# Pooled attention and two MoE layers on one core: which block of the expert stage follows its condition

## The chip, the core and the metric

The kernel runs on one core of one Trainium2 chip. The metric is the device time of one execution in microseconds; several runs are timed and their median is given. A profile is one further execution, recorded by the hardware profiler: its span runs from the first to the last instruction of the program.

## The reference, cut to what matters

Three stages follow one another. Attention with keys and values that are averaged over groups of 8, a dense layer with squared ReLU, and a layer of 8 experts: each of 2304 tokens goes to the expert with the largest logit, up to a capacity of 576 tokens for each expert, and its row is written with a gate weight.

```
logits = x @ w_gate
expert_idx = np.argmax(logits, axis=1)
...
h = np.maximum(np.einsum('ecd,edf->ecf', disp, w1), 0.0)
y = np.einsum('ecf,efd->ecd', h, w2)
...
        out[i] = gate_w[i] * y[expert_idx[i], pos[i]]
```

How many tokens an expert gets is known only when the routing has run, so the program has code for every outcome and picks its way by conditions on registers.

## The kernel before, in words

Attention and the dense layer are planned by a list of steps with priorities (class `Steps`, up to `S_.run()`); they run in 9 chunks of 256 tokens and fill most of the time. The expert stage behind them is written out by hand, in a fixed order on TensorE (PE), VectorE (DVE) and ScalarE (ACT).

An expert is worked in pieces. `fetch` takes the token numbers of a piece from a table and `gather` (L1002) issues an indirect DMA on GpSimd (POOL) for each 128 rows. `y_trans` (its transposes are L1030, its gate copy L1023, its two copies out of PSUM L1032 and L1033) turns the gathered rows into the layout that the multiplications need. `pair` multiplies 256 rows by the first matrix (L1470), applies ReLU, multiplies by the second matrix (`gb`, L1439) and ends in `finish`, which scales the rows and scatters them to the output by an indirect DMA on POOL (`put`, L1428). `trio` is `pair` with 64 rows more, `twins` (L1581 to L1639) takes two small experts at once. `w_load` issues the loads of the next expert's weights on the sync engine (SP, L1066), 7 loads of 512 KB in a row; ACT and DVE split them into two parts (L260, L261).

The first pair of the first expert stands ahead of the condition. It is cut in two: the call `second = pair(0, ..., cut=True)` issues everything up to the first quarter of the second output tile, and returns `second()`, which issues the remaining three quarters, beginning with a `y_trans(0)`. During the first part the routing of the last chunk ends: `finalize` and `line_index` compute the registers, the latter the one at place `R_LINE`, which is 1 when the counts of all experts fit the pattern for which `line()` was written.

Then every engine loads that register (`val`, L993) and branches on it (L1826). Where it is 1 the **straight code** runs: `second()`, a `trio`, and `line()`, which has two small conditions of its own (L1787). Otherwise the **general code** runs: `second()` and `rest()`, a deep tree of conditions with a block for each outcome. With the inputs of this case the straight code runs. Each engine has its own instruction stream in which all these blocks lie one behind another; the general code's are the many, the straight code's the few. `tc.If` takes as `preferred_fallthrough_block` which of its two blocks is laid directly behind the branch. Behind both is the end of the program: SP waits for the last DMAs, each engine drains, and a barrier of all engines closes it (the records with L1902).

Of the kernel before, what the change touches and what calls it, by code (L numbers as in the profile page):

```python
# [43 lines left out]
R_LINE = R_MAX + 1  # L44
# [184 lines left out]
def tile_kernel(ctx: ExitStack, tc: tile.TileContext, q, k, v, w_in, w_out, w_gate, w1, w2, cap, gate_rows, consts, out):  # L229
# [761 lines left out]
    def val(t, i, lo, hi, engines=None):  # L991
        kw = {} if engines is None else {"engines": engines}
        return nc.values_load(t[0:1, i:i + 1], min_val=lo, max_val=hi, **kw)  # L993
# [76 lines left out]
    def w_load(t, r, parts=range(NSTG), after=None):  # L1070

        if after is not None:
            for i in parts:
                nc.vector.tensor_copy(out=st["stg"][i][0:1, 0, 0:1], in_=f(after[0:1, 0, 2 * P - 1:2 * P]))
        e = r if t is None else val(t, r, 0, E - 1, SPE)
        for i in parts:
            w_part(e, i)
# [320 lines left out]
    mp, yg, yh, yl, cur, regs, regse = (st[x] for x in ("mp", "yg", "yh", "yl", "cur", "regs", "regse"))  # L1398
# [259 lines left out]
    def run(kind, r, x, nxt=True, split=None, n=2, part=range(16), extra={}, at=None, third=2):  # L1658

        if at is None:  # L1660
            at = x + 1 if kind is trio else x
        ft = [lambda: fetch(val(regs, 2 * E + r * NU + at, 0, E * NJ - 1, DVE), n, third)]
        sp = [] if split is None else split_list(split, 1 if kind is single else None)
        if kind is not single:
            h = {}
            for i in part if sp else ():
                h.setdefault(SPLITS[i], []).append(sp[i])
            nh = {0: ft, **{(11 if kind is trio else 8) + t: [lambda t=t: y_trans(t)] for t in range(n)}}
        else:
            h = {i: [sp[x] for x in part if a <= x < b] for i, (a, b) in enumerate(zip((0, *SINGLE), (*SINGLE, 16))) if sp}  # L1670
            nh = {0: ft, 4: [lambda: y_trans(0)]}
            if n > 1:
                nh[5] = [lambda: y_trans(1)]
        kind(r % 2, merged(nh if nxt else {}, h, extra))
# [65 lines left out]
    def rest():  # L1740

        nh = halves(0)
        with tc.If(val(regse, 2, 0, 1) < 1):
            with tc.If(nh > 0):
                fetch(val(regse, 1, 0, E * NJ - 1, DVE))
                y_trans(0)
                y_trans(1)
                with tc.If(nh > 2) as two:
                    run(pair, 0, 0, n=3)
                with two.Else():  # L1750
                    run(single, 0, 0)
        w_load(regs, 1)
        with tc.If(nh < 7) as three:
            with tc.If(nh > 4) as odd:
                run(single, 0, 1, True, 1)
            with odd.Else():
                for fn in split_list(1):
                    fn()
        with three.Else():
            many(nh, 0)  # L1760
        any_(1)
        overflow()
# [19 lines left out]
    def line():  # L1782


        for r in (1, 2):
            now = splits(r + 1, {h: [i for i in range(16) if SPLITS[i] == h] for h in range(16)} if r == 1 else W_REST)
            with tc.If(halves(r) > 8, preferred_fallthrough_block=False) as half:  # L1787
                run(trio, r, 0, at=0, extra=now, third=4)
            with half.Else():
                run(pair, r, 0, extra=now)  # L1790
            if r == 1:
                rows = {0: [next_rows(2, 3)], 8: [lambda: y_trans(0)], 9: [lambda: y_trans(1)], 10: [lambda: y_trans(2)]}
            else:
                rows = {0: [two_rows], 8: [y_two]}
            pair(r % 2, merged(rows, splits(r + 2, W_LATE, r == 1)))
        twins(splits(4, W_LAST, False))
# [15 lines left out]
    def ordered(*more):  # L1812
        return tc.manual_schedule(engines={ET.PE, *more})
# [9 lines left out]
            14: [lambda: y_trans(2)],  # L1823
        }, cut=True)
    with ordered(ET.DVE, ET.Activation):
        with tc.If(val(regs, R_LINE, 0, 1) > 0, preferred_fallthrough_block=False) as on:  # L1826
            second()
            run(trio, 0, 1, True, 1, 3, extra={0: [lambda: w_load(regs, 1)]}, third=4)
            line()
        with on.Else():  # L1830
            second()
            rest()
# [74 lines left out]
```

## Time and profile before

| | us |
|---|---|
| median of 3 runs | 683.26 |
| lowest and highest run | 681.84, 683.71 |
| the profiled execution, its own time | 682.42 |
| its span, first to last instruction | 680.7 |
| mean granted TensorE clock | 0.996 of full speed |

The first number is what a change is measured by. The profiled execution is one run; its own time is 1.7 us more than its span, and 0.84 us under the median. Its rows have a time axis that begins at the first instruction. PE is the matmul part of TensorE, PEld its weight loads; a "q" behind an engine's name (PEldq, POOLq) marks records of its sequencer, such as branches, waits and DMA issues, which don't count as busy time. `<-issue` behind an idle time means that the engine waited for no semaphore that the profile shows.

### The profile page before, as it was taken

To read this page: it belongs to the slowest core of one execution; us is meant where nothing else is said; L and a number is where in the kernel's file an instruction comes from. 1 tells how busy PE (TensorE), PEld (TensorE's weight loads), DVE (VectorE), ACT (ScalarE), POOL (GpSimd) and SP (SyncE) were. 2 spreads that over 40 slices of the span, in tenths; PEclk is the share of its full clock that TensorE was granted. 3 is DMA by queue.
4 is the path that set the end of the run, shared out by engine and by line. 5 is a ranking of instruction groups with operands and counts; after the bars stand their busy time and mean duration, and the time that the engine had idled before them with its cause. 6 is when DMAs were issued, how large, how long until landed. Compare 5 with 4: busy or idle time off the path is not lost. (4 is left out here: it accounts for less than half of the span.)

```text
span 680.7 us, 12008 instructions
## 1 busy us (share of the span) xinstructions
PE 666.2 (98%) x4263; PEld 599.2 (88%) x4264; DVE 418.5 (61%) x1127; ACT 328.2 (48%) x904; POOL 195.8 (29%) x230
## 2 busy tenths in 40 slices
PE   7999999999999999999999999999999999999996
PEld 6888889999999999889899899998997989889985
DVE  6998996222188899485379658445354466464352
ACT  5998884344254244354344333243431466453352
POOL 3524543232235233234233133242202211301110
PEclk9999999999999999999999999999999999999999
DMA  8989913010321220010010000062004674655110
GB/s 309 401 321 355 313 61 104 32 48 16 124 63 50 87 78 9 1 55 17 2 48 17 1 32 1 3 221 91 1 33 161 222 245 140 211 153 182 48 59 4
DMA packets 40682, 73.47 MB, mean 108 GB/s; under 512 B 8417, under 2 KB 17889, under 8 KB 40480
## 3 DMA queue, kind: packets, MB, share of 16 engines
q1 hardware_dynamic: 38208, 64.89, 28.1%
q0 software_dynamic: 2400, 7.66, 3.4%
q8 instruction: 38, 0.62, 0.4%
q14 instruction: 36, 0.29, 0.1%
HBM read 59.63 MB, written 13.12 MB: 107 GB/s over the span
## 5 line engine op out<-in xcount | busy, mean ns | idle before, releaser
L735 PE MATMUL h<-xh,W 128*128 128x256 f32 x1152 | 213.6, 284 | 0.4 <-ACT r L740 0.4
L755 POOL TENSOR_TENSOR gl<-r,gh 128x256 fp32r<-128x256 f32 x144 | 117.7, 818 | 271.6 <-ACT gh L751 161.3
L735 PEld LDWEIGHTS h<-xh,W 128*128 128x128 f32 x1152 | 184.3, 189 | 9.9 <-ACT r L740 0.6
L768 PE MATMUL y<-W,gh 128*128 128x512 f32 x576 | 184.9, 402 | 0.4 <-DVE W L319 0.4
L735 PE MATMUL h<-xl,W 128*128 128x256 f32 x576 | 161.8, 281 | 0.0
L740 ACT ACTIVATE r<-h 128x256 f32<-128x256 f32 x144 | 55.2, 383 | 134.6 <-PE h L735 119.0
L747 DVE SCALAR_TENSOR_TENSOR r<-h,r 128x256 f32<-128x256 f32 x131 | 54.9, 419 | 103.5 <-ACT r L740 103.3
L768 PE MATMUL y<-W,gl 128*128 128x512 f32 x288 | 113.6, 395 | 0.9 <-POOL gl L755 0.9
L768 PEld LDWEIGHTS y<-W,gh 128*128 128x128 f32 x576 | 99.4, 189 | 15.7 <-DVE W L319 0.7
L735 PEld LDWEIGHTS h<-xl,W 128*128 128x128 f32 x576 | 109.0, 189 | 0.1
L751 ACT CAST gh<-r 128x256 fp32r<-128x256 f32 x144 | 58.4, 406 | 63.6 <-DVE r L747 63.5
L1470 PE MATMUL hp<-yh,W 128*128 128x256 f32 (+1 forms) x384 | 74.4, 290 | 0.0
L825 DVE SCALAR_TENSOR_TENSOR junk<-ysb,wgb 128x512 bf16<-128x512 f32 x80 | 67.7, 846 | 1.1
L768 PEld LDWEIGHTS y<-W,gl 128*128 128x128 f32 x288 | 54.2, 188 | 14.8 <-POOL gl L755 2.1
L1470 PEld LDWEIGHTS hp<-yh,W 128*128 128x128 f32 x384 | 61.0, 188 | 0.6
L1439 PE MATMUL po<-W,xh_e 128*128 128x512 f32 x192 | 61.4, 401 | 0.0
L1470 PE MATMUL hp<-yl,W 128*128 128x256 f32 (+1 forms) x192 | 55.6, 290 | 0.0
L261 DVE TENSOR_TENSOR W<-stg,W 128x512 fp32r<-128x512 f32 x64 | 42.3, 688 | 12.1 <-ACT W L260 11.2
L1439 PEld LDWEIGHTS po<-W,xh_e 128*128 128x128 f32 x192 | 34.7, 188 | 6.8
L1428 POOL DMA_INDIRECT out_dram<-ysb,sidx x12 | 11.9, 995 | 97.1 <-ACT ysb L1417 83.6
L1476 DVE SCALAR_TENSOR_TENSOR xl_e<-hp,xh_e 128x256 fp32r<-128x256 f32 x48 | 20.1, 421 | 31.2 <-ACT xh_e L1475 27.0
L1439 PE MATMUL po<-W,xl_e 128*128 128x512 f32 x96 | 37.8, 394 | 0.0
(223 smaller groups left out, 921.7 us busy)
## 6 DMA issues: line engine op xcount, KB each, us to landing
stg<-in_moe_w_dram SPq DMA_DIRECT2D x40, 512.0 KB, 5.1
raw<-in_moe_w_in_dram SPq DMA_DIRECT2D x16, 512.0 KB, 8.3
raw<-in_moe_w_out_dram SPq DMA_DIRECT2D x16, 512.0 KB, 7.8
kraw<-in_k_dram SPq DMA_DIRECT2D x16, 288.0 KB, 2.7
out_dram<-zt SPq DMA_DIRECT2D x18, 256.0 KB, 4.9
y_dram<-ysb SPq DMA_DIRECT2D x18, 256.0 KB, 2.2
qT<-in_q_dram SPq DMA_DIRECT2D x16, 256.0 KB, 5.3
vraw<-in_v_dram SPq DMA_DIRECT2D x12, 256.0 KB, 2.7
```

The source lines that it names most:

```text
L261: eng.tensor_tensor(out=lo, in0=src, in1=f(hi), op=ALU.subtract)
L735: nc.tensor.matmul(ps, wt[kk][:, l, o:o + P], r[:, kk, :], start=(n == 0), stop=(n == 3 * KD - 1))
L740: nc.scalar.activation(out=box["r"], in_=box["ps"], func=AF.Relu)
L747: nc.vector.scalar_tensor_tensor(out=r, in0=box["ps"], scalar=0.0, in1=r, op0=ALU.max, op1=ALU.mult)
L751: nc.scalar.copy(out=box["gh"], in_=box["r"])
L755: nc.gpsimd.tensor_tensor(out=box["gl"], in0=box["r"], in1=f(box["gh"]), op=ALU.subtract)
L768: nc.tensor.matmul(st["y", c][t], l[:, ts], r, start=(ff == 0 and n == 0), stop=(ff == NF - 1 and n == 2))
L825: nc.vector.scalar_tensor_tensor(out=junk, in0=st["yb", c, t] if c < 2 else st["ysb", c][t], scalar=1.0, in1=st["wgb"][:, e], op0=ALU.mult ...
L1428: nc.gpsimd.indirect_dma_start(out=out, out_offset=bass.IndirectOffsetOnAxis(ap=sidx[:n, t:t + 1], axis=0), in_=ot[:n], in_offset=None, bo ...
L1439: nc.tensor.matmul(ps, l, r, start=(fi == 0 and x == 0), stop=(fi == 7 and x == 2))
L1470: nc.tensor.matmul(ps, ww[:, l, o], r[:, kk, 0:n2], start=(kk == 0 and x == 0), stop=(kk == KD - 1 and x == 2))
L1476: nc.vector.scalar_tensor_tensor(out=lo, in0=p_, scalar=0.0, in1=f(h), op0=ALU.max, op1=ALU.subtract)
```

## The change

One argument of one condition is turned over. The condition, both blocks and all instructions in them stay as they are; the blocks lie in another order in each engine's stream. Before, the general code is laid behind the branch and the straight code behind all of the general code. After, the straight code is laid behind the branch, and the general code between it and the end of the program.

```diff
     with ordered(ET.DVE, ET.Activation):
-        with tc.If(val(regs, R_LINE, 0, 1) > 0, preferred_fallthrough_block=False) as on:
+        with tc.If(val(regs, R_LINE, 0, 1) > 0, preferred_fallthrough_block=True) as on:
             second()
             run(trio, 0, 1, True, 1, 3, extra={0: [lambda: w_load(regs, 1)]}, third=4)
             line()
```

## Rows read from the trace of the kernel before

**Rows 1.** The page's busy time, share of the span and instructions of each engine.

```profile
PE 666.2 (98%) x4263; PEld 599.2 (88%) x4264; DVE 418.5 (61%) x1127; ACT 328.2 (48%) x904; POOL 195.8 (29%) x230
```

**Rows 2.** Stretches: us, busy us (instructions) by engine, granted clock, DMA share, GB/s.

```profile
core 0: us, PE busy (x) PEld busy (x) DVE busy (x) ACT busy (x) POOL busy (x), PEclk, DMA share, GB/s
517.00:522.00 5.00, 3.76 (x18) 2.83 (x17) 0.15 (x1) 0.69 (x1) 2.91 (x3) 1.00 0.66 191
522.00:672.00 150.00, 150.00 (x902) 133.76 (x901) 76.56 (x183) 71.35 (x154) 23.77 (x24) 1.00 0.47 155
```

**Rows 3.** Timeline around the condition: start us, us, instruction, [idle before <-releaser].

```profile
517.25 0.95 POOL L1002 DMA_INDIRECT yg<-y_dram,gix  x1 [0.30 <-issue]
...
520.02 0.39 PE L1439 MATMUL po<-W,xl_e 128*128 128x512 f32 x1
...
520.88 0.15 DVE L1023 COPY gt<-yg 128x1 f32<-128x1 f32 x1 [4.45 <-issue]
...
521.64 0.63 PE L1030 MATMUL yTp<-cst,yg 128*128 128x128 f32 x4 [1.24 <-issue]
521.77 4.71 SPq L1066 DMA_DIRECT2D stg<-in_moe_w_dram  x7
...
523.27 0.40 PE L1439 MATMUL po<-W,xl_e 128*128 128x512 f32 x1
...
523.51 0.60 PE L1030 MATMUL yTp<-cst,yg 128*128 128x128 f32 x4
```

**Rows 4.** Line L1826, 500 to 530 us: duration ns min/median/max, first and last start.

```profile
L1826 DVEq COMPARE_BRANCH  x1: 72/72/72, 516.9 to 516.9; - x1
L1826 SPq COMPARE_BRANCH  x1: 165/165/165, 517.1 to 517.1; - x1
L1826 PEldq COMPARE_BRANCH  x1: 4107/4107/4107, 517.4 to 517.4; - x1
L1826 ACTq COMPARE_BRANCH  x1: 50/50/50, 520.1 to 520.1; - x1
L1826 POOLq COMPARE_BRANCH  x1: 45/45/45, 520.9 to 520.9; - x1
```

**Rows 5.** Line L993, 515 to 523 us: SP's register loads before and behind the branch.

```profile
L993 SPq TENSOR_LOAD <-regs x2: 278/278/278, 516.5 to 520.5; - x2
```

**Rows 6.** Line L1428, 516 to 528 us: POOL's sequencer before and behind the branch.

```profile
L1428 POOLq MOVE  x2: 29/32/35, 516.3 to 524.0; - x2
```

**Rows 7.** DMA queues, 516.8 to 521.7 us: packets, MB, share of 16 engines.

```profile
q8 instruction: 1, 0.02, 1.7%
q14 instruction: 3, 0.02, 1.4%
```

**Rows 8.** Line L1787, 600 to 617 us: TensorE's branch into the block behind it.

```profile
L1787 PEldq COMPARE_BRANCH  x1: 69/69/69, 607.8 to 607.8; - x1
```

**Rows 9.** DMA queues, 517 to 519.2 us: POOL's indirect DMAs.

```profile
q0 software_dynamic: 90, 0.31, 58.3%
```

**Rows 10.** Line L1428, whole run: its 14 scatters, issue to landing.

```profile
DMA to landing us min/median/max: 2.8/4.5/7.6
```

**Rows 11.** Timeline of the last 12 us: the last work of DVE and POOL.

```profile
675.32 0.48 DVE L1619 SCALAR_TENSOR_TENSOR ysb<-pb,gate,yg 32x256 f32<-32x256 f32 x1 [0.37 <-ACT yg L1618]
676.07 0.93 POOL L1639 DMA_INDIRECT out_dram<-ysb,sidx  x1 [15.95 <-POOLq L1826]
```

**Rows 12.** Line L1826, 660 to 681 us: the branches at the straight code's end.

```profile
L1826 PEldq COMPARE_BRANCH  x1: 179/179/179, 672.3 to 672.3; - x1
...
L1826 DVEq COMPARE_BRANCH  x1: 41/41/41, 675.3 to 675.3; - x1
...
L1826 POOLq COMPARE_BRANCH  x1: 33/33/33, 675.9 to 675.9; - x1
```

**Rows 13.** Line L1902, 670 to 679.9 us: waits and drains of the program's end.

```profile
L1902 SPq EVENT_SEMAPHORE  x9: 28/28/28, 678.5 to 679.0; - x9
...
L1902 DVEq DRAIN  x1: 322/322/322, 675.5 to 675.5; - x1
L1902 POOLq DRAIN  x1: 3743/3743/3743, 676.1 to 676.1; - x1
```

## The prediction, made before the changed kernel ran

> **What bounds the kernel now.** I read the page's busy times first: PE is busy for 666.2 us, 98% of the span, and nothing else comes near [rows 1]. So only what stops PE, or what follows its last multiplication, can be worth anything. The table of stretches then shows where PE stops in the expert stage: not at all from 522 to 672 us (150.00 of 150.00 us busy), but in the five microseconds from 517 to 522 it is busy for only 3.76 us [rows 2]. The timeline of that stretch has the hole: a multiplication of L1439 starts at 520.02, the next work, a transposition, at 521.64, with 1.24 us idle "<-issue", that is, behind no semaphore [rows 3]. The line of the condition explains it: PE's branch is on record for 4107 ns from 517.4 to 521.5 [rows 4]. PE had multiplications queued that lasted until 520.41, and ran dry for the rest.
>
> The other engines stop at the same branch, behind a short record. DVE branches at 516.9 and does its next work at 520.88 [rows 3, 4], 3.9 us later. SP branches at 517.1 (for 165 ns) and loads its next register at 520.5, 3.2 us later [rows 4, 5]. POOL branches at 520.9 and moves on at 524.0, 3.1 us later [rows 4, 6]. In the same stretch the two instruction queues moved four packets [rows 7]. I read this as each engine fetching the code that it jumped to.
>
> **The change at the head.** The straight code now follows the branch, and no engine jumps over anything there. The nearest price for such a branch is that of the small condition L1787 at 607.8 us, which goes on into the block behind it: 69 ns on PE [rows 8]. With it PE's sequencer is free again at 517.5, 2.9 us before its queue is empty, and the queue never runs dry. The gain on PE is counted from start to start, since ends of matmuls are modelled: 521.64 - 520.02 = 1.62 us now; the same pair of lines, where nothing stands between them, needs 523.51 - 523.27 = 0.24 us [rows 3]. The difference is **1.38 us**. It cannot be more: PE has no other hole up to 672 us [rows 2]. It is less if something else is late at that place, so the bounds are 0 and 1.38 us.
>
> What could be late is the gathered rows. The first gather (128 rows of 520 floats, 0.27 MB) is needed at 520.26; by 519.2 the indirect queue had moved 0.31 MB [rows 9], so it is there. The second was issued at 517.25 and is needed at 523.51 - 1.38 = 522.13, 4.9 us after its issue. It now gets company: SP's seven weight loads began at 521.77, 1.3 us after SP came through [rows 3, 5]; with the branch done at 517.3 they begin at about 518.6, amid the gathers. No row shows a gather in exactly that company. The nearest are the 14 scatters of the same queue, which land 2.8 to 7.6 us after issue, 4.5 in the middle [rows 10]. At 4.5 us the second gather lands at 521.75, in time; at 7.6 us it lands at 524.85 and PE waits 2.7 us. I take the middle, cost 0, and keep 2.7 us as the other end. The earlier weight loads bring nothing either: PE never waits for them now [rows 2]. DVE's, ACT's and POOL's stalls go too, but lie beside PE's work.
>
> [...]
>
> **The change at the tail.** What was saved at the head is spent at the end. Today the straight code ends close to the end of the program; PE's last branch takes 179 ns, POOL goes from its branch at 675.9 straight into its drain at 676.1 [rows 12, 13]. Afterwards all of the general code lies between, so each engine's last jump is a far one, and I price it by that engine's own stall at the head, shifting everything by -1.38 us:
> - PE: 672.3 - 1.4 + 4.1 = 675.0.
> - DVE: 675.3 + 0.04 - 1.38 + 3.9 = 677.9.
> - POOL: 675.96 - 1.38 + 3.1 = 677.7 [rows 4, 6, 12].
>
> What ends last today is POOL's drain, from 676.1 for 3.743 us to 679.82 [rows 13]; SP's waits end at 679.0 and DVE is done by 675.9. The question is what the drain waits for. DVE's drain ends at 675.85, 0.05 us behind its last work (675.32 + 0.48 = 675.80) [rows 11, 13]: a drain lasts until the work in flight is over, not for a time of its own. Read so, POOL's drain ends when its last scatter is finished with, at 679.82 - 1.38 = 678.44 whenever it begins, and the three far jumps, all over by 677.9, hide behind it. Cost 0; with PE's 4.1 us instead of POOL's 3.1 it would be 0.3 us. The cover is thin: 0.5 us for DVE, 0.7 us for POOL. The other end is a drain that takes its 3.74 us from its issue: 677.7 + 3.74 = 681.4 against 679.82, +1.6 us net of the gain, or +2.6 us with a stall of 4.1.
>
> [...]
>
> **Sum.** -1.38 (head) + 0 (gathers) + 0 (tail): 682.42 - 1.38 = 681.04 us for an execution like the profiled one, 0.20% less. The median is 0.84 us above that execution, so the forecast for a median is 683.26 - 1.38 = **681.9 us**. A measurement of this kernel can tell about 0.3%, 2.05 us, from no change, so the gain lies below what counts as faster.
>
> **Rivals.**
> - *The forecast* (0.58): head gained, tail covered, 681.9 us.
> - *Late gathers* (0.17): the weight loads that start 3.2 us earlier delay the second gather past 522.13, and PE stands on L1030 again. For it: the scatters that take over 4.9 us. Against it: the middle one doesn't. Time 681.9 + 0 to 2.7, in the middle about 683 us.
> - *The tail is exposed* (0.15, the other side): POOL's drain counts from its issue, behind a far jump. It decides once POOL comes through later than 678.4. For it: POOL's drain lasts 2.8 us beyond the recorded end of its scatter at 677.0 [rows 11, 13], which nothing in the trace explains. Against it: DVE's drain. Time 683.26 + 1.6 = 684.9, up to 685.9 us.
> - *Nothing moves* (0.10): the stall isn't the jump but belongs to the condition (the register, the waits before it), or the block behind must be fetched as well. Against it: L1787 loads a register in the same way and passes in 69 ns [rows 8]; for it: that branch has smaller blocks around it. [...] 683.3 us.
>
> **Numbers.** The predicted time is the forecast's. The runs of before lie between 1.4 us below and 0.5 us above their median, so the forecast's own range is 680.9 to 682.9. The whole range reaches up over the late gathers, over no change and to the lower part of the exposed tail: 680.9 to 684.6; left out are the rest of that tail and the forecast's lowest scatter. No case gives 2.05 us of gain by itself; a fifth of the forecast's chance for scatter makes 0.12 faster. Slower by over 2.05 us is only the upper part of the exposed tail, and the worst gathers: 0.08. The rest, 0.80, is within 0.3%.
>
> **What would show it.** Right: PE's record on L1826 near 0.07 us, no idle time before the first L1030 at 520.3, PE full from 480 us to its end, SP's first L1066 at about 518.6; at the end 3 to 4 us between each engine's last branch and its drain, and POOL's drain short, ending near 678.4. The forecast is wrong if PE waits at the second L1030 (gathers), if POOL's drain is still about 3.7 us long and begins at 677.7 (tail), or if a gap of 3 to 4 us behind L1826 remains at the head (nothing moves).

## The result, and the profile after

The changed kernel is slower: a median of 686.85 us (684.53 to 688.49, 11 runs) against 683.16 us (681.84 to 686.09, 11 runs of the kernel before). The ratio is 1.0052, with an interval of 1.0038 to 1.0066. The forecast was 681.9 us, and the range of 680.9 to 684.6 us doesn't hold the result. The profiled execution took 687.97 us, 1.1 us more than the median, and has a span of 686.2 us. It is set against the profiled execution of before, with 682.42 and 680.7 us.

First the stretches around the condition, in the same columns as [rows 2].

```profile
core 0: us, PE busy (x) PEld busy (x) DVE busy (x) ACT busy (x) POOL busy (x), PEclk, DMA share, GB/s
517.00:522.00 5.00, 5.00 (x26) 4.10 (x25) 0.77 (x7) 0.69 (x1) 3.51 (x4) 1.00 0.52 120
522.00:672.00 150.00, 147.82 (x874) 131.36 (x873) 76.60 (x182) 71.23 (x153) 24.07 (x25) 0.99 0.47 157
```

The hole between 517 and 522 us is gone, as forecast. But the stretch behind it, in which PE used to be full, now lacks 2.18 us, and the granted clock is no longer 1.00 in it. TensorE's timeline shows where.

```profile
521.31 0.39 PE L1439 MATMUL po<-W,xl_e 128*128 128x512 f32 x1
521.55 0.60 PE L1030 MATMUL yTp<-cst,yg 128*128 128x128 f32 x4
...
523.90 0.63 PE L1030 MATMUL yTp<-cst,yg 128*128 128x128 f32 x4 [0.36 <-DMA yg<-y_dram,gix]
...
527.75 0.43 PE L1030 MATMUL yTp<-cst,ysb 64*128 64x64 f32 x4 [1.82 <-DMA ysb<-y_dram,gix]
```

The first rows are transposed 0.24 us behind the start of the multiplication ahead of them; it was 1.62 us [rows 3]. The head has gained its 1.38 us. The second rows then wait 0.36 us and the third 1.82 us, both for a gather. This is the 2.18 us that is missing.

The branches and the weight loads at that place:

```profile
L1826 SPq COMPARE_BRANCH  x1: 157/157/157, 518.4 to 518.4; - x1
L1826 PEldq COMPARE_BRANCH  x1: 92/92/92, 518.7 to 518.7; - x1
...
L1066 SPq DMA_DIRECT2D stg<-in_moe_w_dram x7: 4/342/383, 519.4 to 523.7; - x7
```

PE's branch takes 92 ns instead of 4107 [rows 4]. SP, which also no longer waits behind its branch, begins its weight loads at 519.4, that is 2.4 us earlier than in [rows 3], although PE came to this place 1.3 us later. The third gather was issued 0.45 us behind the first of them. From the timelines, first of the changed kernel, then of the kernel before:

```profile
519.80 0.94 POOL L1002 DMA_INDIRECT ysb<-y_dram,gix  x1 [0.30 <-issue]
```

```profile
518.50 0.95 POOL L1002 DMA_INDIRECT ysb<-y_dram,gix  x1 [0.30 <-issue]
...
525.45 0.46 PE L1030 MATMUL yTp<-cst,ysb 64*128 64x64 f32 x4
```

In the changed kernel the third rows were usable at 527.75, 8.0 us behind the issue of their gather. In the kernel before they were there when PE came to them at 525.45, 7.0 us behind it. Loads and gathers stand in different queues; the profile counts the packets of both against the same 16 DMA engines. In the changed kernel, from 519.4 to 527.7 us (packets, MB, share of the 16 engines; q1 has the loads, q0 POOL's gathers and scatters):

```profile
q1 hardware_dynamic: 440, 1.62, 53.1%
q0 software_dynamic: 285, 0.95, 41.6%
```

Together that is 95% of the engines' time.

Then the clock, in the stretches around 530 us:

```profile
527.80:529.10 1.30, 1.30 (x8) 1.10 (x9) 0.47 (x3) 0.37 (x1) 0.00 (x0) 1.00 1.00 402
529.10:532.50 3.40, 3.40 (x13) 3.15 (x13) 0.10 (x2) 0.69 (x1) 1.00 (x1) 0.50 1.05 408
532.50:534.00 1.50, 1.50 (x12) 1.50 (x11) 0.42 (x1) 0.40 (x2) 0.00 (x0) 0.99 0.66 251
```

For 3.4 us the granted clock is 0.50. PE is busy all the time and gets less done: three multiplications of L1470 take 0.80 us from start to start there (530.02 to 530.82) and 0.45 us behind it (533.35 to 533.80). The kernel before has 1.00 from 522 to 672 us [rows 2].

Last, the end of the program: branches and the first drain of POOL, with POOL's last work between them.

```profile
L1826 PEldq COMPARE_BRANCH  x1: 3753/3753/3753, 676.1 to 676.1; - x1
...
L1826 POOLq COMPARE_BRANCH  x1: 33/33/33, 679.7 to 679.7; - x1
...
679.87 0.93 POOL L1639 DMA_INDIRECT out_dram<-ysb,sidx  x1 [15.95 <-POOLq L1826]
...
L1902 POOLq DRAIN  x1: 2667/2667/2667, 682.7 to 682.7; - x1
```

PE's last branch now takes 3.75 us instead of 179 ns [rows 12]. POOL branches at 679.7 and comes to its drain at 682.7, 3.0 us later. The drain takes 2.667 us and ends at 685.4. It ended at 679.8 [rows 13].

**The account**, from start to start. PE's last group of multiplications (L1610), first before, then after:

```profile
673.67 1.10 PE L1610 MATMUL pb<-W,xl_e 128*128 128x256 f32 x8
```

```profile
677.47 1.10 PE L1610 MATMUL pb<-W,xl_e 128*128 128x256 f32 x8
```

| part | before | after | change |
|---|---|---|---|
| start of the last L1439 ahead of the first rows | 520.02 | 521.31 | +1.29 |
| from there to the first L1030 | 1.62 | 0.24 | -1.38 |
| first L1030 to the last L1610 | 152.03 | 155.92 | +3.89 |
| last L1610 to the end of POOL's drain | 6.15 | 7.89 | +1.74 |

The first line lies ahead of the condition, where the two programs are the same. The experiments have that code too, and with them this L1439 starts anywhere from 519.9 to 521.9 us, so this line is scatter of single runs. The other three make +4.25 us. The medians differ by 3.7 us. Counted from start to start as well, 2.39 of the 3.89 us lie between the first and the third L1030 (6.20 us against 3.81), where the two waits are, and 1.50 us behind the third (149.72 against 148.22), where the clock is at half for 3.4 us.

### The profile page after: what moved, and what is told of

Read it like the earlier page. It is cut to its first block, busy times and chain, and to the rows that moved or that the text cites. A ratio compares the mean times of both kernels' runs of the same rounds, so it can differ in the third digit from the quotient of the medians.

```text
span 686.2 us, 12008 instructions
## 1 busy us (share of the span) xinstructions
PE 667.9 (97%) x4263; PEld 600.9 (88%) x4264; DVE 419.2 (61%) x1127; ACT 327.9 (48%) x904; POOL 195.4 (28%) x230
## 5 line engine op out<-in xcount | busy, mean ns | idle before, releaser
L1470 PE MATMUL hp<-yh,W 128*128 128x256 f32 (+1 forms) x384 | 75.3, 293 | 0.0
L1470 PEld LDWEIGHTS hp<-yh,W 128*128 128x128 f32 x384 | 62.0, 191 | 0.7
L1439 PE MATMUL po<-W,xh_e 128*128 128x512 f32 x192 | 61.6, 402 | 0.0
L1470 PE MATMUL hp<-yl,W 128*128 128x256 f32 (+1 forms) x192 | 56.1, 292 | 0.0
L1439 PEld LDWEIGHTS po<-W,xh_e 128*128 128x128 f32 x192 | 34.7, 188 | 6.8
L1428 POOL DMA_INDIRECT out_dram<-ysb,sidx x12 | 11.9, 994 | 97.6 <-ACT ysb L1417 83.0
L1439 PE MATMUL po<-W,xl_e 128*128 128x512 f32 x96 | 38.0, 396 | 0.0
```

The costliest lines, as they stand in the source:

```text
L1428: nc.gpsimd.indirect_dma_start(out=out, out_offset=bass.IndirectOffsetOnAxis(ap=sidx[:n, t:t + 1], axis=0), in_=ot[:n], in_offset=None, bo ...
L1439: nc.tensor.matmul(ps, l, r, start=(fi == 0 and x == 0), stop=(fi == 7 and x == 2))
L1470: nc.tensor.matmul(ps, ww[:, l, o], r[:, kk, 0:n2], start=(kk == 0 and x == 0), stop=(kk == KD - 1 and x == 2))
```

## The experiments

**Theory A** after this reading: the weight loads start so early that they share the DMA engines with the gathers, the gathers come late, PE idles and its clock falls; at the end a far jump delays POOL's drain, which takes 2.7 us of its own. The rivals stand with each run. The kernel before was timed on the same chip beside each. The ratio on record is not the quotient of the two medians; where the two differ in a way that matters, both are given. Edits shift the line numbers of the experiments by a few.

**The weight loads behind the rows** (new layout):

```diff
         with tc.If(val(regs, R_LINE, 0, 1) > 0, preferred_fallthrough_block=True) as on:
             second()
-            run(trio, 0, 1, True, 1, 3, extra={0: [lambda: w_load(regs, 1)]}, third=4)
+            w_load(regs, 1, after=yl)
+            run(trio, 0, 1, True, 1, 3, third=4)
```

> The changed kernel, but SP's seven weight loads behind the condition wait until VectorE has written the second rows' low parts (one 1x1 copy into each buffer makes them wait), so they start behind the gathers. Theory (early loads delay the gathers, the idle time lowers the clock, the far jump at the end delays POOL's drain): TensorE goes from L1439 to each of the three L1030 within 0.4 us, the granted clock stays 1.00 from 517 to 560 us, the head gain of 1.4 us is kept, the tail still costs 1.7 us: 0.3 us above the kernel before, ratio 1.000 to 1.002, about 3.4 us under the changed kernel. Rival (the rows are late for another reason of the new order of blocks): TensorE still waits over 1 us at the second or third L1030, and the time stays near 686.9 us.

683.05 us against 682.86 us, ratio 1.0006 (0.9996 to 1.0016). The transpositions in the timeline, then the stretch behind them, the line of the loads and the drain:

```profile
520.70 0.60 PE L1030 MATMUL yTp<-cst,yg 128*128 128x128 f32 x4
...
522.53 0.60 PE L1030 MATMUL yTp<-cst,yg 128*128 128x128 f32 x4
...
524.46 0.46 PE L1030 MATMUL yTp<-cst,ysb 64*128 64x64 f32 x4
...
522.00:672.00 150.00, 150.00 (x902) 133.75 (x902) 77.24 (x190) 70.92 (x155) 23.73 (x24) 1.00 0.46 156
...
L1066 SPq DMA_DIRECT2D stg<-in_moe_w_dram x8: 12/360/1062, 526.7 to 538.2; - x8
...
L1903 POOLq DRAIN  x1: 2668/2668/2668, 678.3 to 678.3; - x1
```

With the loads at 526.7 us no transposition waits (from 519.4 to 527.7 us the loads now take 1.8% of the DMA engines' time instead of 53.1%), and the granted clock is 1.00 from 522 to 672 us. From the first L1030 to the last L1610 (672.65) it takes 151.95 us: all of the 3.89 us is gone, by moving the loads alone. The tail is left: from the last L1610 to the end of the drain 8.28 us, 2.1 us more than before. So the tail's price eats up the head's gain (+2.1 and -1.4 us in the trace, 1.0006 in the time), and the early loads are what makes the change a clear loss.

**The early loads alone, in the old layout:**

```diff
-            7: [..., lambda: fetch(val(regs, 2 * E, 0, E * NJ - 1, DVE), 3), line_index],
+            7: [..., lambda: fetch(val(regs, 2 * E, 0, E * NJ - 1, DVE), 3), line_index,
+                lambda: w_load(regs, 1)],
...
-            run(trio, 0, 1, True, 1, 3, extra={0: [lambda: w_load(regs, 1)]}, third=4)
+            run(trio, 0, 1, True, 1, 3, third=4)
```

> The kernel before, its order of blocks unchanged, but the seven weight loads stand ahead of the condition, so that SP issues them beside the gathers. Theory (early loads delay the gathers): TensorE waits 1 to 3 us at the second or third L1030, behind the 4 us branch that is still there, perhaps a stretch of lower clock behind it; time 1 to 4 us above before. Rival (the order of the blocks itself makes the rows late): no wait at L1030 beyond the branch, time as before within 0.3%.

686.77 us (685.18 to 688.3) against 682.86 us, ratio 1.0055 (1.0035 to 1.0076): as much as the whole change, without it. The place was missed: the loads began at 515.5 us, ahead of all gathers (517.6 to 520.1), and already the first rows came late.

```profile
525.98 0.63 PE L1030 MATMUL yTp<-cst,yg 128*128 128x128 f32 x4 [3.93 <-DMA yg<-y_dram,gix]
...
L1827 PEldq COMPARE_BRANCH  x1: 6327/6327/6327, 519.0 to 519.0; - x1
...
526.80:530.20 3.40, 3.40 (x12) 2.71 (x11) 0.75 (x2) 0.96 (x2) 0.00 (x0) 0.50 0.84 313
```

The granted clock falls again for 3.4 us. PE's branch over the general code takes 6.3 us here instead of 4.1 [rows 4]. It ends at 525.3, so 3.3 of the 3.93 us of idle time would have been there without the late rows, which add 0.6. The early loads thus slowed both: the gathers (7.7 to 8.0 us from issue to landing) and what the engines do at the branch. SP and POOL, too, stop for 5.9 and 5.8 us behind it, where it was 3.2 and 3.1. That code and loads compete for the DMA engines fits, but was not shown by itself.

**The hint: the old layout, with the branch marked as likely taken.** The call `tc.mark_branch_hint_location` names the branch, by its label, ahead of the condition; in the kernel's text this announcement stands right behind `line_index`, for all five engines.

```diff
-            7: [..., lambda: fetch(val(regs, 2 * E, 0, E * NJ - 1, DVE), 3), line_index],
+            7: [..., lambda: fetch(val(regs, 2 * E, 0, E * NJ - 1, DVE), 3), line_index,
+                lambda: tc.mark_branch_hint_location("straight", hint="LikelyTaken", engines=[ET.PE, ET.DVE, ET.Activation, ET.Pool, ET.SP])],
...
-        with tc.If(val(regs, R_LINE, 0, 1) > 0, preferred_fallthrough_block=False) as on:
+        with tc.If(val(regs, R_LINE, 0, 1) > 0, preferred_fallthrough_block=False, label="straight") as on:
```

> The kernel before, its order of blocks unchanged, with a branch hint (likely taken) for the condition on all five engines; it stands at the start of the main block. If the hint has each engine fetch the straight code ahead: TensorE's record on L1826 falls from 4.1 us to under 0.8 us and the tail stays as before; then by the theory the weight loads start early as in the changed kernel and the rows come late: 1.4 us gained, 2 to 4 us lost in waits and clock, some 1 to 2.5 us above before. Rival (rows are late for another reason): 1.4 us below before. If a hint so far ahead does nothing: as before within 0.2%, record of 4.1 us.

682.2 us (680.2 to 683.27) against 682.86 us, ratio 0.9982 (0.997 to 0.9995): a little faster than the kernel before, with an interval that just leaves out 1 (the quotient of the medians is 0.9990). A loss of 1 to 2.5 us was expected, so that part was a miss.

```profile
L1827 PEldq COMPARE_BRANCH  x1: 390/390/390, 518.7 to 518.7; - x1
...
525.84 0.43 PE L1030 MATMUL yTp<-cst,ysb 64*128 64x64 f32 x4 [0.39 <-DMA ysb<-y_dram,gix]
```

The branch takes 390 ns instead of 4107, and the straight code still lies at the end of the program, so no jump is paid there. What is left of the trouble with the loads is 0.39 us at the third rows: SP's first load came at 520.14, 0.25 us behind the issue of the third gather (519.89), where in the changed kernel it came 0.45 us ahead of it. The third rows were usable 6.0 us behind their issue instead of 8.0. This shift of 0.7 us in the loads is what the expectation had not seen.

**The hint, and the loads behind the rows:** the two edits above together, in the old layout.

> Old layout with the branch hint, and the weight loads behind the gathered rows. Theory A (the head's stall is the fetch of the target, the loads delay the gathers, the far jump at the end costs on POOL): all gain, no price. PE's record on the condition 0.4 us or less, head -1.4 us; all three gathers land within 4 us of issue and no L1030 waits (the run with the hint alone waited 0.4 us at the third); granted clock 1.00; POOL's drain as before, some 3.7 us from about 674.7. Ratio 0.998 (0.997 to 0.999), about 681.4 us. Rival 1, the rows are late simply because they are wanted 1.4 us earlier, not because of the loads: the third L1030 still waits 0.3 to 0.5 us, ratio 0.9985. Rival 2, the hint fetches code at the cost of the gathers' own transfers: the gathers take over 5 us and nothing is gained over the run with the hint alone.

682.75 us (680.82 to 683.58, 12 runs) against 682.49 us, ratio 0.9991 (0.998 to 1.0003): the least certain of the results. 0.998 was expected; the interval holds 1, and the quotient of the medians, 1.0004, lies on its other side, so no gain in time is shown. The trace of the expert stage is as expected:

```profile
517.00:522.00 5.00, 5.00 (x23) 4.08 (x23) 0.93 (x7) 0.69 (x1) 2.95 (x4) 1.00 0.41 100
522.00:672.00 150.00, 150.00 (x904) 133.73 (x903) 77.71 (x190) 71.63 (x154) 24.79 (x25) 1.00 0.46 158
...
L1904 POOLq DRAIN  x1: 3766/3766/3766, 676.5 to 676.5; - x1
```

PE is full from 517 to 672 us, no rows wait, the drain begins with the last scatter. From the first L1030 to the last L1610 (674.07) it takes 151.95 us, and from there to the end of the drain 6.17 us, so the expert stage is 1.4 us shorter than before. What hides it lies at the other end of the program. From 13 to 22.5 us, first in the kernel before and then in this one:

```profile
13.00:22.50 9.50, 7.52 (x38) 6.71 (x37) 9.37 (x23) 8.51 (x19) 3.17 (x4) 0.82 1.06 364
```

```profile
13.00:22.50 9.50, 7.47 (x33) 6.42 (x32) 9.37 (x24) 7.62 (x18) 2.81 (x4) 0.64 1.06 369
```

In all eight profiles whose start-up is on record the clock falls there: for about 3.4 us (a mean of 0.82 over these 9.5 us) in the kernel before, the changed one and three that follow below (the control, the second try of the drain, the far jump made early), for about 6.8 us with the hint alone and here (0.64) and with the loads behind the rows in the new layout (0.69, and 0.96 in the 13 us ahead of it). PE came to the condition 1.86 us later in this profile than in that of before (last L1439 at 521.88 against 520.02). The clock can be a part of that; the rest of the start-up varies as well. Grouped after the fact by the mean clock of the whole run, this kernel has 4 runs at 0.995 or more with a median of 680.84 us (before 682.41, 21 runs), and 8 runs below with 682.93 us (before 683.54, 8 runs). Whether the edit itself makes the longer fall more likely stays open: both of these profiles with the hint show it, but so does one of the six without it (the loads behind the rows in the new layout), and with the hint alone 7 of 10 runs are at 0.995 or more.

**Control: the loads behind the rows in the old layout, without the hint.**

> Control: the kernel before with nothing but the weight loads moved behind the gathered rows. Theory A: in the old layout the loads already began after the gathers had landed, so nothing moves: PE's record on the condition 4.1 us, 1.2 us idle ahead of the first rows, ratio 1.000 (0.999 to 1.001). Rival, the later loads are what the run with the loads behind the rows owes its time to, in either layout: ratio 0.998 or below (gathers and code come sooner), or above 1.001 (weights come late and PE waits on them).

682.5 us, ratio 1.0000 (0.9991 to 1.0009). PE's branch takes 4047 ns and the first L1030 waits 1.18 us, as before. Where the loads start behind the gathers anyway, moving them was worth nothing; they cost something where they start beside the gathers (the 3.89 us of the changed kernel) or ahead of them (1.0055).

**The drain, first try.** Four subtractions on POOL were put behind the last scatter (old layout), so that it comes late to its drain without a jump.

> The kernel before with four subtractions of 128x256 (about 0.82 us each) on POOL behind the last scatter; their result is not used. The jump at the end stays a near one. Theory (POOL's drain takes about 2.7 us of its own, counted from when POOL comes to it): the drain begins about 3.3 us later and lasts 2.6 to 2.8 us, so the span ends about 3.2 us later, ratio 1.0047. Rival, and the prediction's reading (the drain lasts until the scatter is finished with): the drain ends within 0.2 us of the last subtraction, about 680.4, and the span grows by some 0.5 us.

682.69 us, ratio 0.9998 (0.9987 to 1.0009), and a miss of the experiment: the subtractions read nothing that comes late and ran at 656.20 us, 20 us ahead of the scatter. The drain took 3840 ns, from 676.3. It says nothing of the drain.

**The drain, second try:** the subtractions read the rows that DVE writes last.

```diff
+        for i in range(4):
+            nc.gpsimd.tensor_tensor(
+                out=xh[1][0:n, 256 * i:256 * i + 256], in0=hs[0][0:n, 0:256], in1=hs[0][0:n, 256:512], op=ALU.subtract
+            )
```

> The kernel before, with four idle subtractions on POOL (about 0.74 us each) that read DVE's last result and stand behind the last scatter, so that POOL comes to its drain about 3 us later with no jump in between. Theory A, the drain behind a scatter takes about 2.7 us of its own once POOL comes to it: it starts near 679.1 and lasts 2.6 to 2.8 us, end near 681.8, +2.0 us. Rival 1, the reading of the prediction (the drain lasts until the scatter is finished with, at 679.8): it lasts under 1 us and ends by 679.9, +0.1 us. Rival 2, it takes 3.74 us from its issue whatever went before: end near 682.8, +3.0 us. All against the span of before; the medians should move by the same.

685.96 us, ratio 1.0045 (1.003 to 1.006).

```profile
677.11 0.93 POOL L1639 DMA_INDIRECT out_dram<-ysb,sidx  x1 [15.95 <-DVE ysb L1619]
678.05 2.77 POOL L1644 TENSOR_TENSOR xh_e<-ysb 96x256 fp32r<-96x256 f32 x4
...
L1906 POOLq DRAIN  x1: 6237/6237/6237, 677.2 to 677.2; - x1
```

The drain's record begins as soon as the sequencer reaches it (677.2, with the subtractions still to come), not at 679.1 as expected: that part was a misreading of what the record's start means. Its end is what counts, 683.4, which is 2.6 us behind the end of the last subtraction (678.05 + 2.77 = 680.82). The reading of the prediction, an end with the work in flight, would have put it by 680.9; 3.74 us would have been 681.0 from the start of the record, or 684.6 from the end of the subtractions. From the last L1610 (674.71) to the end of the drain it takes 8.74 us, +2.6 us where theory A had +2.0: the subtractions only start when the scatter has left the engine (678.05 behind 677.11 + 0.93). The medians moved by 3.5 us; there are only four runs, all with a mean clock below 0.995, and against the runs of the kernel before of that kind (683.54) it is 2.4 us. With the kernel before (677.00 to 679.82, 2.8 us) and the changed kernel (2.67 us from the moment that POOL reaches it, the engine idle since 680.80) this makes one reading for these three cases: POOL's first drain ends 2.6 to 2.8 us behind the later of the engine's last work and the sequencer's arrival.

**The far jump made early** (new layout, loads behind the rows): the last scatter stands in a second condition of its own behind the first, so that POOL jumps over the general code early, while it has nothing to do (it branches at 657.5 us). The scatter's row numbers lie in a buffer that outlives the block; that edit is not shown.

```diff
-        twins(splits(4, W_LAST, False))
+        return twins(splits(4, W_LAST, False))
...
-            line()
+            last = line()
...
+        with tc.If(val(regs, R_LINE, 0, 1) > 0, preferred_fallthrough_block=True):
+            last()
```

> The new layout with the loads behind the rows, and the last scatter moved out of the straight block to a second condition behind it, so that POOL makes its far jump while it has nothing to do. Theory A: the tail's +1.75 us comes from POOL's far jump between its last scatter and its drain; with the jump made early the drain starts right behind the scatter and lasts about 3.7 us as before, so of the 1.75 us some 1 us or more comes back: PE's end -1.4 us against before, tail at most +0.9 (one register and one branch more), ratio 0.998 to 0.9995. Rival 1, it is PE's or DVE's far jump that the end waits for: the tail stays at +1.75 us or more, ratio 1.0006 or above. Rival 2, the added condition costs a fetch of its own (another record of 3 to 4 us on POOL ahead of the scatter, now with the scatter itself behind it): +2 us or more, ratio 1.002.

682.46 us against 682.49 us, ratio 1.0007 (0.9996 to 1.0018).

```profile
L1905 POOLq DRAIN  x1: 4578/4578/4578, 675.1 to 675.1; - x1
```

Inconclusive. POOL's far jump did leave the path, and the drain begins with the last scatter again. But it ends at 679.7, 3.6 us behind the end of that scatter (675.16 + 0.93 = 676.09) and not 2.8. From the last L1610 (672.23) to the end of the drain it is 7.45 us, +1.3 us against before where 0.9 at most was expected. 0.5 us of this is that the scatter starts later behind the second condition (2.9 us behind the last L1610 instead of 2.4); why the drain is 0.8 us longer stays open. Of the 2.1 us that the tail costs with the loads behind the rows, 0.8 us came back.

**Idle time and the clock.** Two kernels from the one with the hint and the loads behind the rows: on POOL one small and three, or six, subtractions stand ahead of the third gather, so that PE idles at the third rows with no weight load beside the gathers. The gather overwrites what they compute. The call, not shown, passes `late=3` or `late=6`. If idle time lowers the clock, the second kernel should show it and the first, whose wait is planned shorter than that of [rows 3], should not; if it takes the loads beside the rows, neither should.

```diff
-    def fetch(col, n=2, third=2):
+    def fetch(col, n=2, third=2, late=0):
...
         rows_of(col, n, third)
         for t in range(n):
+            if t == 2 and late:
+                a, b, cur = got(2)[:, 0:256], got(2)[:, 256:512], st["gix"].bitcast(F32)
+                nc.gpsimd.tensor_tensor(out=b[:, 0:3], in0=cur[:, 0:3], in1=cur[:, 0:3], op=ALU.subtract)
+                for i in range(late):
+                    nc.gpsimd.tensor_tensor(out=a, in0=a, in1=b, op=ALU.subtract)
             gather(t)
```

> The kernel with the hint and the loads behind the rows, with one small and three 128x256 subtractions on POOL (about 0.75 us each) ahead of the third gather, so that the third rows come some 2.5 us later than without them and no weight load stands in that stretch. Worked out: the third gather goes out at 520.4 + 2.5 = 522.9, lands 3.6 us later at 526.5, is wanted at 525.9: PE idles about 0.6 us at the third L1030 (0 to 1.3). [...]

One run, 683.21 us; a single run of the kernel before beside these two took 684.49 us, so their times say little and the traces are compared. The third rows, in PE's timeline, and the stretch around them:

```profile
525.92 0.43 PE L1035 MATMUL yTp<-cst,ysb 64*128 64x64 f32 x4 [0.68 <-DMA ysb<-y_dram,gix]
...
522.00:672.00 150.00, 149.32 (x898) 133.15 (x897) 77.72 (x190) 71.75 (x154) 25.74 (x27) 1.00 0.48 157
```

The clock is 1.00, and from the first transposition (521.41) to the last L1610 group (674.11) it takes 152.70 us: 0.75 us more than 151.95, the idle time and no more.

> The same with six subtractions: the third gather goes out at 520.4 + 4.8 = 525.2, lands at 528.8, PE idles about 2.9 us (2 to 4) at the third L1030; the weight loads still stand behind those rows. Theory A: the idle time alone lowers the clock: granted 0.5 for 3.4 us beginning 1 to 2 us after PE takes up work again, and 1.4 to 1.5 us are lost in addition to the idle time. Rival (the loads beside the rows lowered it in the changed kernel): clock 1.00 from 517 to 560, and PE's shift behind the wait equals the idle time.

One run, 687.79 us. The same line, and two stretches around it:

```profile
527.88 0.66 PE L1035 MATMUL yTp<-cst,ysb 64*128 64x64 f32 x4 [2.93 <-DMA ysb<-y_dram,gix]
```

```profile
527.00:533.80 6.80, 5.92 (x20) 5.25 (x21) 1.14 (x11) 1.06 (x2) 1.00 (x1) 0.50 0.62 204
533.80:560.00 26.20, 26.20 (x152) 23.47 (x152) 17.28 (x42) 15.24 (x36) 3.92 (x4) 1.00 0.83 282
```

The clock fell at 527.0, still within the idle time and ahead of the first weight load (529.5), so it fell with no weight load beside it. It stayed at 0.50 for 6.8 us, twice as long as in the changed kernel, and it began earlier than expected. From 521.13 to 678.70 are 157.57 us, 5.62 us more than 151.95: 2.93 us of idle time and 2.7 us for the clock. An idle time of 1.24 us [rows 3] (clock 1.00 from 522 us on [rows 2]) or 1.18 us (the control, ratio 1.0000) cost only itself; one of 1.82 us (the changed kernel), 2.93 us, and 3.93 us (the early loads) cost 1.5, 2.7 and 1.6 us more. The large dose is one execution.

## Why the prediction was wrong, point by point

- **The head was right.** -1.38 us was forecast from [rows 3] and -1.38 us came, with PE's record at 92 ns (69 forecast). That the stall belongs to the jump is borne out by the hint, which takes the record from 4107 to 390 ns in the old layout with no block moved. That it is the fetch of the target fits the instruction queues, with four packets behind the condition in the kernel before [rows 7] and none from 517 to 522 us in the changed one. The rival "nothing moves" is out. PE's far branch took 4.1 us at the head and, in the changed kernel, 3.75 us at the end.
- **"I take the middle, cost 0" for the gathers failed first.** The scatters' 4.5 us [rows 10] were taken for gathers that now have seven loads of 512 KB beside them, though the text itself said that no row shows a gather in that company. The third gather took 8.0 us, just beyond the slow end of 7.6 us. The price of the rival, 0 to 2.7 us, holds the 2.18 us that PE waited. The place was wrong: the second gather was watched, and PE idled 0.36 us for it; the third, issued 0.45 us behind the first load, cost 1.82 us. It was never given a due time in the working. By the same method it was due at 525.45 - 1.38 = 524.07, 5.6 us behind its issue at 518.50, and the slow end of 7.6 us would have made PE wait 2.0 us there.
- **The clock was missing.** Neither the sum nor a rival had it that PE's clock can fall with a wait of its own. In this kernel a wait of 1.24 us stands in [rows 3] without a fall, and behind the one of 1.82 us the granted clock was 0.50 from 529.1 to 532.5 us, which brought 1.5 us on top. The trace of before has a fall too: at start-up PE waits 1.41 us ahead of L627 at 15.19, and the clock is 0.50 from 15.9 to 19.3 us. By it the upper end for the gathers, a wait of 2.7 us, should have been given a surcharge.
- **"A drain lasts until the work in flight is over" failed at the tail.** It was read off DVE's drain and moved to POOL. POOL's has 2.6 to 2.8 us of its own, so the far jump, well forecast for PE (4.1, measured 3.75) and POOL (3.1, measured 3.0) and too long for DVE (3.9, measured 2.9), could hide behind nothing. The tail cost 1.74 us in the changed kernel and 2.1 us with the loads behind the rows. The row that said so was quoted in the rival: the drain's 2.8 us behind the scatter's end, "which nothing in the trace explains". The rival's own size, 3.74 us from the issue, was too much by 1.1 us, since that record contains the scatter.
- **The rivals were right, but as alternatives.** Late gathers and the exposed tail were given 0.17 and 0.15 and priced one at a time; both happened in the same run. They hang on the same cause, engines that come through earlier at the head and later at the end, and a case with both belonged on the list: 681.9 + 2.4 + 1.5 + 1.7 = 687.5 us, against a median of 686.85.

The jump saved at the head is paid at the end. PE's far branch moved from 517.4 us (4107 ns) to 676.1 us (3753 ns), the instruction queues moved no packet from 674 us on in the kernel before and 8 from 675 us on in the changed one, and the kernel with the loads behind the rows, whose only loss is at the end, comes out at 1.0006.

## What to carry to other kernels

A block laid behind its branch only moved the jump here (PE's 4107 ns at the head became 3753 ns at the end): ask which end of the block has cover for a jump of 3 to 4 us, and announce the branch instead where that is possible (in the traces the announcement took 1.0 to 1.4 us off the expert stage; in the times less of it shows). Where a stall goes, list each transfer that now starts earlier and give every load that is needed next (all of them, not the first) a due time against it; if PE bounds the kernel and can be made to wait longer than the 1.2 us that cost nothing extra here, add what its clock may lose (1.5 to 2.7 us in the three cases here). And read an unexplained remainder behind the last work, like the 2.8 us of the drain, as a cost that will be paid again, not as cover.

## What was not expected of the hardware

- POOL's first drain at the program's end ends 2.6 to 2.8 us after POOL is done (3.6 us in one case that stays open). On the other engines, which also came to their drains with no work left, the drains at the changed kernel's end are on record for 7 to 81 ns.
- With weight loads under way the jump over the same code took longer: PE's far branch took 4.1 us without and 6.3 us with them (one profile with them).
- Where a fall of the clock is on record ahead of the program's end, it was low for about 3.4 us or 6.8 us: in the start-up of eight profiles, and around the idle times of 1.82, 2.93 and 3.93 us in the expert stage (3.4, 6.8 and 3.4 us). With the idle time of 2.93 us it fell before work resumed (527.0 against 527.88), in the changed kernel 1.4 us after (529.1 against 527.75).
